# Expert 0's layers gathered ahead of batch 1, with its W2 and batch 1's q and k loads in another order

## The chip, the cores and the metric

The kernel runs on one core of one Trainium2 chip. The metric is the device time of one launch in microseconds (us). The kernel before was run three times: 1004.11, 1004.98 and 1006.6 us, median 1004.98.

## The reference

Two stages, all inputs in float32. First, sliding-window attention with a linear bias: 8 batches, 8 heads, 576 positions, 64 per head, a window of 128. Then a dense mixture of experts over the 4608 tokens of 512: every token goes through all 8 experts, and the gate's weights are balanced over rows and columns eight times.

```python
# attention, per batch and head
scores = q @ k.T / sqrt(64) - slope[h] * abs(i - j)      # only 0 <= i - j < 128
x[:, h] = softmax(scores) @ v                             # x: 4608 x 512
# mixture of experts
P = exp(x @ w_gate - max)                                 # 4608 x 8
repeat 8 times: P /= rowsum + 1e-9; P /= colsum + 1e-9; P *= 4608 / 8
out = sum over e of P[:, e] * (relu(x @ w1[e]) @ w2[e])   # w1: 512 x 1024, w2: 1024 x 512
```

## The kernel before

The kernel is one long program without loops on the chip: Python loops write every instruction in order, and each engine runs its own in that order, waiting on semaphores where data or a buffer isn't ready. It has two large parts. In the first, attention of the 8 batches is computed, and experts 0 and 1, which need no gate, are woven into it on TensorE as a filler. In the second, the gate is balanced and experts 2 to 7 are computed. The change touches the first part alone, and there the first two batches.

**Attention.** A batch has 4 full blocks of 128 positions and a tail of 64; each block is done in two half steps (`u`), four heads each, so a batch is ten half steps. `steps` lists them all; the main loop runs one half step each time round and already issues the scores, exps and masks of the next. In a half step TensorE makes the scores (`scores`, L438; both halves of a block together), ScalarE their exp (`exps`, L444), VectorE multiplies by the mask (`masks`, L449), TensorE multiplies by v (`values`, L472), VectorE takes the reciprocal of the sums (L482) and scales into `xsb` (L483). When a block is done, `turn_x` transposes x for the experts on TensorE (L510; batches 0 to 2 and 7), ScalarE or VectorE copies it out of PSUM (L519, L521), and `keep_x` stores x to memory (L498), at most three blocks late; that copy of x is read only in the second part.

**q, k and v.** `load_qk` loads q and k of a batch on SP's queue (L282; four loads of 512 KB for batches 1 and 2). `cast_qk` makes float16 of one of four head pairs `j`: k on ScalarE (L300), q on VectorE (L298), or both on POOL (L296). `turn_pe` then transposes on TensorE (L368), and ScalarE or VectorE copies k and q into place (L383, L381). `load_v` (L391) and `cast_v` (L403, L404, on POOL) bring one block of v each; v's raw tiles and the tails (`load_tail`, L271) share five buffers. In batch 0 three junk matmuls (`spin`, L260) go ahead of each `values`, and `spin_alone` adds some in other places.

**Experts 0 and 1.** `load_weights` loads W1 (L100) and W2 (L102) of an expert on POOL's queue. `unit_atoms` cuts a unit of two or four blocks of x into atoms: eight of layer 1 (four matmuls, L117, and a relu out of PSUM on ScalarE, L129; on alternating engines, L125 and L129, for blocks 0 to 3 of expert 0), and one atom of layer 2 for each block (eight matmuls, L141; two atoms of four for blocks 0 to 3 of expert 0). The result leaves PSUM on VectorE (`keep`: L553 for blocks 0 to 3 of expert 0, L559 for others). `order` lists the units; in the kernel before, expert 0's blocks 0 to 3 are two units of two blocks, all others have four.

`Filler` hands the atoms out. `take` gives out one, `fill(us)` several by an assumed cost of 0.87 us for each layer 1 atom of four blocks and 1.74 for a block of layer 2. `ready` says how many blocks of x exist, `allowed` which experts may start, and while `hold` is set no atom of layer 2 is given out. In the main loop a half step's share of the backlog is its `budget`; batch 0 has none. Between batches 0 and 1 (`nxt == (1, 0, 0)`) the loop gives out atoms by `take`, around the casts and turns of batch 1; between batches 1 and 2 it uses `fill`.

All PSUM tiles of this part other than scores come from one tag, `pmm`, with four banks: layer 1, layer 2, values, turns and gates share them.

**What sets the order around the change.** SP's queue, before: all of batch 0's loads, then q and k of batch 1 (L282), block 0 of v and the tail of batch 1, then one block of v for each finished block, with stores of x among them. POOL's queue, before: casts of v of batch 0 with W1 of expert 0 and the gate's weights among them, two casts of q of batch 1 (pairs 2 and 3), then W2 of expert 0, then casts of v of batch 1 as they land, with the weights of expert 1 at half step 5 of batch 0. `hold` is lifted at half step 2 of batch 1.

Of the kernel before, what the change touches and what calls it, by code (L numbers as in the profile page):

```python
# [14 lines left out]
def kernel(  # L15
# [10 lines left out]
    nc = tc.nc  # L26
# [4 lines left out]
    B, H, S, Dh = q.shape  # L31
# [5 lines left out]
    NBLK = Ntok // P  # L37
    NDT = HD // P
    NFT = Fd // P
    GT = 512  # L40
    NG = Ntok // GT
    NKB = 5
    RI = 4
# [18 lines left out]
    xd = nc.dram_tensor("xd", [NBLK, P, HD], FP16, kind="Internal").ap()  # L62
# [107 lines left out]
    L1_US, L2_US = 0.87, 1.74  # L170
# [62 lines left out]
    if True:  # L233
# [42 lines left out]
        def load_qk(b, parts=1):  # L276
            q32 = per.tile([P, H, RI * Dh], FP32, name=f"q32_{b}", tag="a8", bufs=8)
            k32 = per.tile([P, H, RI * Dh], FP32, name=f"k32_{b}", tag="a8", bufs=8)
            w = H // parts
            for n in range(parts):  # L280
                for t, src in ((q32, q), (k32, k)):
                    nc.sync.dma_start(  # L282
                        out=t[:, n * w : n * w + w],
                        in_=src[b, n * w : n * w + w, 0:SM, :].rearrange("h (p i) d -> p h (i d)", i=RI),
                    )
            raw[b] = (q32, k32)
# [126 lines left out]
        def sizes(kb):  # L413
            return P if kb < NKB - 1 else TL
# [85 lines left out]
        def turn_x(b, kb):  # L500
            nk = sizes(kb)
            blk = 4 * b + kb if kb < NKB - 1 else 4 * B + b // 2
            lo = 0 if kb < NKB - 1 else TL * (b % 2)
            xT, at = x_of(blk)
            to = xT[:, at, :, lo : lo + nk]
            xsb = xsbs.pop((b, kb))
            if by_pe(b):
                ps = aps.tile([P, NDT, P], FP16, name=f"psX_{b}_{kb}", tag="pmm", bufs=4)
                for j in range(NDT):
                    nc.tensor.matmul(  # L510
                        out=ps[:, j, 0:nk],
                        lhsT=xsb[0:nk, 2 * j : 2 * j + 2, :],
                        rhs=ident[0:nk, 0:nk],
                        is_transpose=True,
                        start=(j == 0),
                        stop=(j == NDT - 1),
                    )
                if b == 0:
                    nc.scalar.copy(out=to, in_=ps[:, :, 0:nk])  # L519
                else:  # L520
                    nc.vector.tensor_copy(out=to, in_=ps[:, :, 0:nk])  # L521
            else:
                nc.sync.dma_start(out=to, in_=xsb[0:nk].rearrange("p h d -> p (h d)"), transpose=True)
            kept.append((blk, lo, nk, xsb))
            keep_x(3)

        def gates(b0, b1):
# [31 lines left out]
            nc.vector.tensor_copy(out=yo, in_=ps)  # L559
            stores.append((e, blk, yo))  # L560

        order = [(0, 0, 2), (0, 2, 2)]
        for b0 in range(RI, NBLK, 4):
            order += [(0, b0, 4), (1, b0 - 4, 4)]
        order.append((1, NBLK - 4, 4))
        filler = Filler(
# [89 lines left out]
        load_first()  # L656
        spin_alone(20)
        make_mask(range(4))
        load_qk(1, 2)
        load_v(NKB)  # L660
        load_tail(1)
        cast_v(0)
        load_weights(0, 0, 1)
        cast_v(1)
# [11 lines left out]
        cast_v(2)  # L676
        nc.gpsimd.dma_start(out=wg_sb, in_=moe_w_gate.rearrange("(dt p) e -> p dt e", p=P))
        cast_v(3)
        cast_v(4)
        for j in (2, 3):  # L680
            cast_qk(1, j, (0,), True)
        load_weights(0, 1, 2)
        cast_qk(0, 2)
        cast_qk(0, 3)
        spin_alone(4)
# [8 lines left out]
        for n, (b, kb, u) in enumerate(steps):  # L694
            nxt = steps[n + 1] if n + 1 < len(steps) else None
            at = 2 * kb + u
            left = ((10 - at) % 10 + 1) if b >= XPE else 10 - at + 9 * (at == 9)
            budget = filler.backlog() / (11 if (b, at) == (XPE, 0) else left)
            if b == 0:
                budget = 0.0  # L700
            if nxt:
                if nxt[0] < XPE and nxt[1:] == (RI - 2, 1):
                    turn_pe(nxt[0], 0, NDT)
                if nxt == (1, 0, 0):
                    filler.ready = RI
                    spin_alone(6)
                    for _ in range(NFT):
                        filler.take()
                    cast_qk(1, 0)
                    cast_qk(1, 1)  # L710
                    for j in range(NDT):
                        turn_pe(1, 1, j)
                        turn_pe(1, 0, j)
                        if j < 2:
                            cast_qk(1, j + 2, (1,))
                        filler.take()
                if nxt == (2, 0, 0):
                    filler.fill(8.5)
                    cast_qk(2, 0)
                    cast_qk(2, 1)  # L720
                    filler.fill(2.5)
                    for j in range(NDT):
                        turn_pe(2, 1, j)
                        turn_pe(2, 0, j)
                        if j < 2:
                            cast_qk(2, j + 2, (1,))
                        filler.fill(1.0)
                if n == 0:
                    scores(*nxt)
                elif nxt[2] == 0 and nxt[1] < NKB - 1:  # L730
                    scores(*nxt)
                    scores(*nxt[:2], 1)
                if nxt[1] < NKB - 1:
                    exps(*nxt)
            if nxt and nxt[1] < NKB - 1:
                masks(*nxt)
            got = filler.fill(1.0) if b else 0.0
            if (b, kb, u) == (1, 1, 0):
                spin_alone(8)
            values(b, kb, u)  # L740
            if n > 0 and u == 0 and by_pe(steps[n - 1][0]):
                turn_x(*steps[n - 1][:2])
            if u == 1 and n // 2 + NKB < B * NKB:
                cast_v(n // 2 + NKB)
            filler.fill(budget - got)
            if at == 0 and b >= XPE:
                turn_tail(b)
            if at == 0 and b > XPE:
                filler.ready = 4 * b
            if at < 8 and b < XPE:  # L750
                filler.ready = 4 * b + at // 2
            if at == 8 and b < XPE:
                filler.ready = 4 * b + 4
            if u == 1 and not by_pe(b):
                turn_x(b, kb)
            if u == 1:
                if kb == 1 and b > 0:
                    gates(4 * b - 4, 4 * b)
                if n // 2 + NKB + 1 < B * NKB:
                    load_v(n // 2 + NKB + 1)  # L760
            if b == 0 and at == 5:
                load_weights(1)
            if (b, at) == (1, 8):
                filler.allowed.add(1)
            if (b, at) == (1, 5):
                for j in (2, 3):
                    cast_qk(2, j, (0,), True)
            if (b, at) == (1, 2):
                filler.hold = False
            if (b, at) == (0, 9):  # L770
                load_qk(2, 2)
            if (b, at) == (0, 7):
                homes(1)
            if (b, at) == (1, 3):
                homes(2)
            if 1 <= b < B - 2 and at == 3:
                load_qk(b + 2)
            if XPE <= b + 1 < B - 1 and at >= 8:
                cast_qk(b + 2, at - 8, (1,), True)
                cast_qk(b + 2, at - 8, (0,))  # L780
            if XPE <= b + 1 < B:
                if at == 0 and b + 1 == XPE:
                    for j in range(2):
                        cast_qk(b + 1, j, (1,), True)
                        cast_qk(b + 1, j, (0,))
                if at < 2:
                    cast_qk(b + 1, at + 2, (1,), True)
                    cast_qk(b + 1, at + 2, (0,))
                if at == 1:
                    store(1)  # L790
                    turn_qk(b + 1)
                    order_qk(b + 1, 1, range(NDT))
                if at == 5:
                    cast_tail(b + 1)
                if at in (6, 7):
                    order_qk(b + 1, 0, range(2 * at - 12, 2 * at - 10))
            if b < B - 1 and at == (1 if b > 1 else 5) and b:
                load_tail(b + 1)
            if 10 * b + at >= 66:
                i = 10 * b + at - 66  # L800
                if i % 8 == 0:
                    home_last(2 + i // 8)
                (load_w2 if i % 8 < 4 else load_w1)(2 + i // 8, i % 4, 4)
            if (b, at) == (7, 0):
                todo += sums_of(2, *extras(2))
            if b == 7 and at >= 5:
                some(1)
# [450 lines left out]
```

## Time and profile before

| | before |
|---|---|
| runs, us | 1004.11, 1004.98, 1006.6 (median 1004.98) |
| profiled execution, us | 1004.29 |
| its span, us | 1002.5 |
| TensorE busy, us | 989.1 |
| VectorE / ScalarE / POOL busy, us | 762.1 / 717.8 / 104.7 |
| granted TensorE clock | 1.00 |
| bytes moved by DMA | 122.46 MB, mean 122 GB/s |

The profile is of one execution; its span runs from the first to the last instruction, and 1.8 us of the run lie around it. Engines are PE (TensorE matmuls), PEld (TensorE weight loads), DVE (VectorE), ACT (ScalarE), POOL (GpSimd) and SP (which only issues DMAs). Lines of the order of time read: start, duration, engine, line of the kernel, operation, result tile <- operand tiles, shapes, count, and in brackets the idle time before it with what ended it. Durations of matmuls are those of single ones with their pipeline, so a run's length divided by its count gives the pace. A row "A <- B" in the waits means that A waited for B. In DMA views q1 is the queue that SP's loads and stores use, and q0 that of POOL's.

### The profile page before, as it was taken

What the parts mean: (1) busy time and instruction counts of PE and PEld (TensorE: products, weight loads), DVE (VectorE), ACT (ScalarE), POOL (GpSimd) and SP (SyncE); (2) the same over time, 40 slices, a digit from 0 to 9 for tenths busy, and PEclk for the clock granted to TensorE, in tenths of its full rate; (3) what the DMA queues carried; (4) which work ended last, traced back from release to release, by engine and by line L of the source; (5) the groups of instructions that cost most, each with busy time, mean ns of one, the idle gap of its engine ahead of it and who ended that gap; (6) DMA issues with size and microseconds to landing.
All of it is one profiled execution on the core that took longest, in us unless ns stands there. A gap on an engine that the chain in (4) does not pass through costs nothing.

```text
span 1002.5 us, 27939 instructions
## 1 busy us (share of the span) xinstructions
PE 989.1 (99%) x11591; PEld 801.5 (80%) x11591; DVE 762.1 (76%) x1598; ACT 717.8 (72%) x1216; POOL 104.7 (10%) x182
## 2 busy tenths in 40 slices
PE   7999999999999999999999999999999999999998
PEld 5645544445544899999999999999999999999997
DVE  6737676666688989887887887787787787787787
ACT  7654554555334768888888888888888888888885
POOL 3314344336010000000000000000000000000000
PEclk9999999999999999999999999999999999999999
DMA  9998788889998324324333334434433333433361
GB/s 250 212 261 226 158 217 225 216 182 191 237 187 170 75 50 99 79 61 98 80 64 96 80 70 86 85 68 84 87 82 66 96 75 67 99 75 65 96 117 48
DMA packets 264432, 122.46 MB, mean 122 GB/s; under 512 B 201969, under 2 KB 255729, under 8 KB 264305
## 3 DMA queue, kind: packets, MB, share of 16 engines
q1 hardware_dynamic: 249568, 102.68, 44.7%
q0 software_dynamic: 14304, 17.84, 10.6%
q8 instruction: 90, 1.47, 0.6%
q14 instruction: 38, 0.30, 0.1%
q10 hardware_dynamic: 432, 0.16, 0.1%
HBM read 78.30 MB, written 23.59 MB: 102 GB/s over the span
## 4 chain that ended last, share of the span: by engine, by line
PE 91%; DMA 3%; DVE 3%; ACT 1%; issue 0%; SPq 0%; POOL 0%; DVEq 0%
PE psM L1029 31%; PE psB L992 14%; PE psh L117 12%; PE psy L141 11%; PE psA L992 9%; PE psC L992 9%; DMA v<-in_v_dram 2%; PE psN L472 1%; PE psS L438 1%; DMA xT<-xsb 1%; PE psT L368 1%; DVE pt L449 0%; DMA q<-in_q_dram 0%; PE psG L531 0%; PE psh L971 0%
## 5 line engine op out<-in xcount | busy, mean ns | idle before, releaser
L1029 PEld LDWEIGHTS <-hs 128*128 128x128 f16 x2996 | 271.0, 98 | 22.4 <-DVE hs L1009 0.4
L1029 PE MATMUL psM<-w2l,hs 128*128 128x256 f16 x1440 | 186.6, 273 | 0.2 <-DVE hs L1009 0.2
L992 PEld LDWEIGHTS <-w1l 128*128 128x128 f16 x2848 | 181.4, 98 | 4.9 <-issue 0.5
L1005 ACT ACTIVATE hs<-hs 128x512 f16<-128x512 f16 x212 | 130.4, 630 | 35.3 <-DVE hs L1175 25.4
L1175 DVE TENSOR_TENSOR hs<-psB,s5y 128x512 f16<-128x512 f32 x106 | 73.3, 692 | 98.5 <-ACT xs L901 92.9
L992 PEld LDWEIGHTS <-s 128*128 128x128 f16 x2136 | 141.7, 98 | 6.4
L129 ACT ACTIVATE hT<-psh 128x512 f16<-128x512 f32 (+1 forms) x144 | 84.0, 586 | 78.9 <-PE psh L117 78.9
L117 PE MATMUL psh<-xT,w1t 128*128 128x512 f16 (+1 forms) x608 | 137.4, 368 | 2.5 <-DMA xT<-xsb 2.5
L901 ACT ACTIVATE xs<-xtok,L_sb 128x512 f16<-128x512 f16 x204 | 136.3, 721 | 1.8 <-DMA xset<-xs 1.8
L141 PE MATMUL psy<-w2t,hT 128*128 128x512 f16 x576 | 135.3, 379 | 0.0
L1029 PE MATMUL psM<-more,hs 128*128 128x256 f16 x864 | 129.5, 273 | 0.0
L992 PE MATMUL psA<-xset,w1l 128*128 128x128 f16 x1424 | 108.6, 219 | 0.0
L992 PE MATMUL psB<-xset,s 128*128 128x128 f16 x1424 | 108.6, 219 | 0.0
L444 ACT ACTIVATE pt<-psS 128x1024 f16<-128x1024 f32 x64 | 64.5, 1021 | 58.1 <-PE psS L438 57.6
L141 PEld LDWEIGHTS <-hT 128*128 128x128 f16 x576 | 53.5, 98 | 59.4 <-issue 1.7
L117 PEld LDWEIGHTS <-w1t 128*128 128x128 f16 x608 | 55.2, 98 | 55.4 <-issue 3.8
L1009 DVE TENSOR_TENSOR hs<-hs 128x1024 f16<-128x1024 f16 x107 | 73.9, 691 | 19.8 <-ACT hs L1005 17.7
L1166 ACT COPY psC<-psB 128x512 f32<-128x512 f32 x106 | 60.4, 570 | 38.8 <-PE psB L992 38.8
L449 DVE TENSOR_TENSOR pt<-pt,mask 128x1024 f16<-128x1024 f16 x64 | 49.2, 769 | 40.7 <-ACT pt L444 40.7
L559 DVE CAST yo<-psy 128x512 f16<-128x512 f32 x65 | 44.5, 689 | 44.7 <-PE psy L141 41.5
L1158 ACT COPY s5y<-psC 128x512 f32<-128x512 f32 x106 | 62.2, 587 | 22.7 <-PE psC L992 22.7
L1073 DVE TENSOR_TENSOR acc<-acc,psM 128x256 f32<-128x256 f32 (+1 forms) x162 | 73.9, 502 | 0.3
(127 smaller groups left out, 1421.0 us busy)
## 6 DMA issues: line engine op xcount, KB each, us to landing
s5y<-ysp SPq DMA_DIRECT2D x36, 256.0 KB, 3.0
ysp<-yo SPq DMA_DIRECT2D x65, 128.0 KB, 3.7
v<-in_v_dram SPq DMA_DIRECT2D x32, 256.0 KB, 4.7
out_dram<-acc SPq DMA_DIRECT2D x31, 256.0 KB, 2.5
q<-in_q_dram SPq DMA_DIRECT2D x5, 1024.0 KB, 6.5
k<-in_k_dram SPq DMA_DIRECT2D x5, 1024.0 KB, 8.8
xtok<-xd SPq DMA_DIRECT2D x34, 128.0 KB, 2.3
w2t<-in_moe_w_dram POOLq DMA_DIRECT2D x4, 1024.0 KB, 11.9
```

The lines of the kernel that those rows point to most:

```text
L117: nc.tensor.matmul(out=ps[:, 0:nt], lhsT=w1ts[e][:, dt, P * ft : P * ft + P], rhs=xT[:, at : at + nb, dt, :], start=(dt == 0), stop=(dt == ...
L129: nc.scalar.activation(out=st["hT"][:, ft, 0:nt], in_=ps[:, 0:nt], func=AF.Relu)
L141: nc.tensor.matmul(out=ps, lhsT=st["hT"][:, ft, P * ms : P * ms + P], rhs=w2ts[e][:, ft, :], start=(ft == 0), stop=(ft == NFT - 1),)
L444: nc.scalar.activation(out=pt, in_=ps.rearrange("p a y n -> p (a y) n"), func=AF.Exp, scale=scale)
L901: nc.scalar.mul(out=xs[2 * (n % 2) + m], in_=xtok[m], mul=P_sb[:, blk, e : e + 1])
L992: nc.tensor.matmul(out=ps[:, j, :], lhsT=q[k][:, P * j : P * j + P], rhs=xset[n % 2][:, x, P * k : P * k + P], start=(start and j == 0 and ...
L1005: nc.scalar.activation(out=h[n][:, slot], in_=src, func=AF.Relu)
L1009: nc.vector.tensor_tensor(out=t[:, 4:6], in0=t[:, 0:2], in1=t[:, 2:4], op=ALU.add)
L1029: nc.tensor.matmul(out=Ms[bk][:, half, :], lhsT=h[n][:, LEFT[m], f, :], rhs=W2L[e][RIGHT[m]][:, f, :], start=(e == 2 and f == 0 and half = ...
L1073: nc.vector.tensor_tensor(out=a, in0=a, in1=p2, op=op)
L1158: nc.scalar.copy(out=s5, in_=pc)
L1175: nc.vector.tensor_tensor(out=h[n][:, 3], in0=pb, in1=s5, op=ALU.add)
```

## The change

`order` now starts with expert 0's blocks 0 to 7 in four units of two blocks and expert 1's blocks 0 to 3 in one unit of four. W2 of expert 0 is asked for after the cast of block 3 of v of batch 0. q and k of batch 1 are no longer loaded at the start: at half step 7 of batch 0 SP gets a store of block 3 of x, which reads `xsb`, and behind it q and k of batch 1, blocks 0 and 1 of v, the tail and blocks 2 and 3 of v. POOL casts q's pairs 2 and 3 there; at half step 9 come the casts of v of batch 1, with the weights of expert 1 after the first two, and two more loads of v. The `turn_x` of that block of x no longer puts it in line for a store. Between batches 0 and 1 sixteen atoms are taken instead of eight, that is layer 1 of blocks 0 to 3; `hold` is lifted there; layer 2 of blocks 0 and 1 follows, then batch 1's turns with half a block of layer 2 after every second one.

```diff
-            kept.append((blk, lo, nk, xsb))
+            if (b, kb) != (0, RI - 1):
+                kept.append((blk, lo, nk, xsb))
...
-        order = [(0, 0, 2), (0, 2, 2)]
-        for b0 in range(RI, NBLK, 4):
+        order = [(0, 0, 2), (0, 2, 2), (0, 4, 2), (0, 6, 2), (1, 0, 4)]
+        for b0 in range(2 * RI, NBLK, 4):
             order += [(0, b0, 4), (1, b0 - 4, 4)]
...
         make_mask(range(4))
-        load_qk(1, 2)
-        load_v(NKB)
-        load_tail(1)
         cast_v(0)
...
         cast_v(3)
+        load_weights(0, 1, 2)
         cast_v(4)
-        for j in (2, 3):
-            cast_qk(1, j, (0,), True)
-        load_weights(0, 1, 2)
...
                     filler.ready = RI
                     spin_alone(6)
-                    for _ in range(NFT):
+                    for _ in range(2 * NFT):
                         filler.take()
+                    filler.hold = False
+                    filler.fill(2 * L2_US)
                     cast_qk(1, 0)
                     cast_qk(1, 1)
                     for j in range(NDT):
...
-                        filler.take()
+                        if j % 2:
+                            filler.take()
...
-            if u == 1 and n // 2 + NKB < B * NKB:
+            if u == 1 and b and n // 2 + NKB < B * NKB:
                 cast_v(n // 2 + NKB)
...
-                if n // 2 + NKB + 1 < B * NKB:
+                if b and n // 2 + NKB + 1 < B * NKB:
                     load_v(n // 2 + NKB + 1)
-            if b == 0 and at == 5:
+            if (b, at) == (0, 2 * RI - 1):
+                nc.sync.dma_start(out=xd[RI - 1], in_=xsbs[0, RI - 1].rearrange("p h d -> p (h d)"))
+                load_qk(1, 2)
+                load_v(5)
+                load_v(6)
+                load_tail(1)
+                load_v(7)
+                load_v(8)
+                for j in (2, 3):
+                    cast_qk(1, j, (0,), True)
+            if (b, at) == (0, 9):
+                cast_v(5)
+                cast_v(6)
                 load_weights(1)
+                load_v(9)
+                load_v(10)
+                for m in (7, 8, 9):
+                    cast_v(m)
...
-            if (b, at) == (1, 2):
-                filler.hold = False
```

`load_v(m)` and `cast_v(m)` count blocks through all batches, five to a batch: 5 to 9 are those of batch 1, 10 the first of batch 2.

## The prediction

> All times are microseconds of the one profiled execution of the kernel before (span 1002.5, whole run 1004.29, so 1.8 lies around the span). The median of the three runs shown is 1004.98, 0.7 above that run; I add my difference to the median. 0.3%, or 3 us, is about what a measurement of this kernel can tell from no change.
>
> **What bounds the kernel.** First the page: busy shares and the 40 slices.
>
> ```profile
> PE 989.1 (99%) x11591; PEld 801.5 (80%) x11591; DVE 762.1 (76%) x1598; ACT 717.8 (72%) x1216; POOL 104.7 (10%) x182
> ...
> PE   7999999999999999999999999999999999999998
> ```
>
> TensorE is busy 99% of the span. The built instruction orders of the two kernels show the same matmuls from the start of batch 3 on, so all the change can alter is what TensorE loses between 10 and 100 us. Busy is not full pace, though. So I read full-pace prices from the chain of waits and count the work of a stretch: a 256-column matmul of layer 1 is 0.110 (28 in 3.07), a 512-column one 0.216 (32 in 6.91), one of layer 2 0.216 (8 in 1.73), a q-and-k turn of one head pair 0.45, the scores of two half steps 0.54, the values of a half step 0.24, gates 0.38. Then the order of time on TensorE:
>
> ```profile
> 24.31 3.66 PE L117 MATMUL psh<-xT,w1t 128*128 128x256 f16 x32
> 28.51 0.70 PE L368 MATMUL psT<-ident,c 128*128 128x128 f16 x8 [0.55 <-ACT c L300]
> ...
> 32.62 0.70 PE L438 MATMUL psS<-qN,kN 64*128 64x256 f16 x8
> ...
> 39.39 1.04 PE L141 MATMUL psy<-w2t,hT 128*128 128x512 f16 x4
> ...
> 44.54 0.41 PE L472 MATMUL psN<-v,pt 128*128 128x65 f16 x8
> ...
> 49.27 1.89 PE L141 MATMUL psy<-w2t,hT 128*128 128x512 f16 x8
> 50.99 7.07 PE L117 MATMUL psh<-xT,w1t 128*128 128x512 f16 x32
> ```
>
> Layer 1 of expert 0 begins at 24.31, scores of batch 1 at 32.62, layer 2 only at 39.39 (W2, asked for at 28.36, landed at 39.2), and batch 1 is through at 49.27. From 24.31 to 50.99 the work is 7.0 (layer 1) + 6.9 (layer 2) + 2.0 (turns) + 2.2 (scores) + 2.2 (values) + 1.2 (spins) + 1.1 (turns of x) + 0.4 (gates) = 23.0, the elapsed time 26.7: **3.7 lost**. The windows view shows why the busy share hides it, and where else to look:
>
> ```profile
> 24.30:51.00 26.70, 25.41 (x302) 17.91 (x301) 20.44 (x50) 15.60 (x27) 8.55 (x20) 1.00 1.07 217
> 51.00:69.30 18.30, 18.30 (x111) 9.13 (x111) 6.64 (x11) 10.06 (x18) 2.69 (x7) 1.00 1.10 279
> 69.30:91.10 21.80, 21.39 (x198) 11.18 (x198) 13.07 (x31) 12.93 (x18) 6.08 (x13) 1.00 0.82 199
> ```
>
> Columns: elapsed, PE, PEld, DVE, ACT, POOL, granted clock, DMA share, GB/s. In the first stretch VectorE is 20.4 of 26.7 busy: attention's latency chain (exp 1.02, mask 0.69, reciprocal and scaling 0.6) is the limit, TensorE waits in small bits. From 51 to 69 TensorE is at full pace. From 69 to 91 about 1.65 is lost again (elapsed 21.8, work 20.2): exps queue behind eight evictions of 0.60, then a VectorE burst without a gap from 76.1 to 84.5. The whole prize is 3.7 + 1.65 = 5.3.
>
> **The change, part by part.**
>
> *Loads.* POOL now issues W2 of expert 0 at about 17.2 (after the cast of block 3 of v, before the wait for block 4) instead of 28.36. SP issues the store of x block 3 at 23.5 (its second half is written by 23.47), then the four q and k loads from 24.0 (0.5 each, as their rows show) instead of 13.2; v, tails and batch 2's loads follow. The DMA view:
>
> ```profile
> q1 hardware_dynamic: 1840, 1.59, 110.2%
> ...
> q0 software_dynamic: 608, 0.62, 73.0%
> q1 hardware_dynamic: 608, 0.61, 44.1%
> ```
>
> The first line is 22.5 to 27 us: q and k alone move 1.59 MB in 4.5 us, 354 GB/s. The other two are 53 to 58: weights (q0) and loads of SP (q1), both backlogged, move the same number of packets. W2 follows W1, which landed at 22.0; 1024 packets at 151 per us (755 in the window 31 to 36) are 6.8: about 28, needed at 31.3. q and k need 2.1 MB / 354 = 5.9 after a start near 25.8, plus 2 shared with W2: about 33.7; the last part is needed at 36. Both are covered, by some 2 to 3 us. v of batch 1 follows by 36 to 38 (needed from 41), expert 1's weights are asked for at about 37 instead of 40.58 and needed from 59; q and k of batch 2 land near 60 and are needed at 68. The delayed stores of x are read only by the last stage. The added wait is SP's, for VectorE's scaling at 23.47; behind it stand all those loads. On POOL the casts of q wait for their loads, and behind them stand the casts of v of batch 1 and expert 1's weights, which have the covers just named. Cost: 0, or one for one what a load is late (first rival). One term: block 4 of v landed at 22.49 beside W1, and now has W2 behind W1 as company; TensorE waits for it at 22.96. I take +0.2 (0 to 0.6).
>
> *Transition.* After layer 1's start come 64 matmuls of 0.110 (7.0) and 16 of layer 2 (3.45): 10.5. VectorE's order is then: evict block 0, evict block 1, cast q. The second eviction (0.69) starts when TensorE is done, the cast (0.56, from the row of two in 1.12) follows, so q's first turn waits 1.2 less 0.22 of k's turn and 0.1 of overlap: **0.9 lost, a new stall** where the old one of 0.55 was. Four turns (1.8), two halves of block 2 (1.73) and 0.2 for a PSUM bank: scores begin 15.1 after layer 1's start, against 8.3 now, for 6.94 more work: -0.1.
>
> *Batch 1.* From the first scores to the end of its last turn of x: now 16.65 for 14.2 of work, 2.45 lost. After the change 1.7 of filler is gone from the gaps between the third and fifth values (the listing shows none there). The chain of exp, mask and scaling stays: walking it with the rows' durations, the values of the sixth half step come 11.1 after the first scores (11.9 now). Then fillers return: eight 0.39 evictions on ScalarE share it with an exp of 1.02, while four PSUM banks are held by values waiting for VectorE: 0.4 lost; 7.95 to the end. Sum 19.05 for 15.95 of work, 3.1 lost: +0.65. Bounds: at batch 0's pace (7.4 from its second block's scores to the sixth values, mine 8.3) the term is -0.25, and -0.65 without the bank wait; at today's pace (9.1) and one exp (1.02) more in the way, +2.45. I keep the walk, whose pace lies between.
>
> *Two-block units.* 64 x 0.110 = 7.02 against 32 x 0.216 = 6.91: +0.1. ScalarE has 16 evictions of 0.386 for 8 of 0.598, +1.4; in the second unit each (0.39) fits under 0.44 of matmuls.
>
> *Batch 2.* Its layer 1 of expert 1 now runs ahead of the scores, so the exps no longer queue behind eight evictions, but the four casts of q of batch 3 still fall on VectorE in one go. Of 1.65 lost I take back 0.6 (between all of it, -1.65, and a worse burst, +0.3).
>
> Sum: +0.2 - 0.1 + 0.65 + 0.1 - 0.6 = **+0.25**, so 1004.5 in the profiled run's terms, 1005.3 on the median. All low ends together (the 0.9 and the bank wait gone too) give -3.2, all high ends +3.4.
>
> **Rivals.**
>
> *q and k come late (slower).* In the rows of before these 512 KB loads took 11.8 (q) and 12.0 (k) from issue to landing, and 16.0 for k beside expert 1's weights. The last is issued at 25.7: at 12 it lands at 37.7, at 16 at 41.7. It decides from 36 on: ScalarE must cast it (0.62) for the third turn, and TensorE, in order, waits one for one: +2.3 to +6.3, say 4, 1009. Against: then 2 MB of weights or four v blocks ran beside them; now one third of W2.
>
> *TensorE's rate falls in the thin half steps (slower).* From the third values to block 3's scores TensorE has 2.6 of work in some 4.5 us, without the spins that batch 0 has. The first 20 spins of the kernel took 3.77, 0.19 each against 0.11 later: one such spell costs 3.77 x (1 - 0.11/0.19) = 1.6, 1006.9. [...] Against: batch 0, with gaps of 0.81 and 0.55, shows a granted clock of 1.00, and no gap that I find is over 1 us.
>
> *The chain contracts (faster).* If batch 1 runs at batch 0's pace and the burst at 76 dissolves: 0.2 - 0.1 - 0.25 + 0.1 - 1.65 = -1.7; without the stall of 0.9 and the bank wait -3.0: 1003.3 to 1002.0. For: VectorE is the limit there and gets the same work in a longer time. Against: q's cast stands behind two evictions in its order.
>
> *The change doesn't do what it says* is excluded for the order (the listing shows W2, the store and the loads in their new places); W2 after 31.3 is priced like the first rival.
>
> **How the numbers follow.** Forecast 0.66, late loads 0.14, rate 0.06, contraction 0.14. Faster by over 3 us is half of the contraction and 0.01 of the forecast: 0.08. Slower by over 3 us is nearly all of late loads (0.13) and the forecast's high end (0.03): 0.16. The rest, 0.76, is within 0.3%. The range from 1002.4 to 1008.6 takes in the forecast's bounds but for the corners and the rate; it leaves out the far half of the contraction (0.07) and of late loads (0.07).
>
> **What would show it.** Right: layer 2 starting within 0.2 of the end of layer 1's 64 matmuls, without a wait for W2; a wait of 0.7 to 1.1 before the first q turn, put down to VectorE's cast; scores of batch 1 near 39.5; its end near 58.6; batch 3's first scores within 1 us of before. Wrong: TensorE waiting for a cast of k or POOL's cast of q; a granted clock under 1.00; batch 1 lasting under 17.5 or over 21 from its first scores.

## The result, and the profile after

The changed kernel ran 1011.77, 1014.13, 1017.11, 1010.92 and 1012.2 us: median 1012.2, where five runs of the kernel before gave a median of 1005.99. By the medians the change is slower by 6.2 us. The ratio with its 95% interval is 1.0083 (1.0066 to 1.01). It is an estimate of its own and not the quotient of the two medians (1.0062); by it the change is slower by 6.6 to 10 us. I forecast 1005.3 and a range from 1002.4 to 1008.6: the result lies outside it. The profiled execution (1011.77) has a span of 1009.9, 7.4 more than that of before.

The page of the changed kernel, the lines that answer to those of before:

```profile
PE 993.0 (98%) x11623; PEld 806.3 (80%) x11623; DVE 763.4 (76%) x1598; ACT 719.3 (71%) x1224; POOL 106.8 (11%) x182
...
PE   8989999999999999999999999999999999999998
```

TensorE is busy 3.9 us longer for the same work (the units of two make 32 matmuls more of half the size, and some matmuls ran slower) and idle 3.5 us longer. A slice is 25.2 us; the third, 50 to 76 us, has an 8 where the page of before has a 9. The order of time on TensorE there (columns as before):

```profile
24.96 7.15 PE L117 MATMUL psh<-xT,w1t 128*128 128x256 f16 x64
31.95 3.62 PE L141 MATMUL psy<-w2t,hT 128*128 128x512 f16 x16
...
37.09 0.84 PE L368 MATMUL psT<-ident,c 128*128 128x128 f16 x12 [1.30 <-DVE c L298]
...
40.88 0.61 PE L438 MATMUL psS<-qN,kN 64*128 64x256 f16 x8
...
52.40 1.03 PE L117 MATMUL psh<-xT,w1t 128*128 128x256 f16 x8 [1.20 <-DVE xT L521]
...
61.22 0.39 PE L510 MATMUL psX<-ident,xsb 128*128 128x128 f16 x4
62.78 1.47 PE L117 MATMUL psh<-xT,w1t 128*128 128x256 f16 x12 [1.18 <-DVE xT L521]
```

Up to 36 us it went as forecast: 64 matmuls of layer 1, layer 2 right behind them, no wait for W2. The stall of q's first turn came, at 1.30. New are the waits of **layer 1 for L521**: VectorE's copy of an x that TensorE has only just turned. Of TensorE's waits from 24 to 125 us it is the longest in total, and the kernel before has none of it:

```profile
PE psh L117 <- DVE xT L521: 3.6, 3, 1.2
```

The second such wait closes batch 1: x is turned by 61.6, the copy that layer 1 needs ends at 62.74. VectorE's own order shows what the copy stands behind:

```profile
61.18 0.69 DVE L560 CAST yo<-psy 128x512 f16<-128x512 f32 x1 [1.03 <-PE psy L141]
61.79 0.16 DVE L482 RECIPROCAL rden<-psN 64x4 f32<-64x4 f32 x1
61.98 0.42 DVE L483 TENSOR_TENSOR xsb<-psN,rden 64x256 f16<-64x256 f32 x1
62.33 0.41 DVE L521 COPY xT<-psX 128x512 f16<-128x512 f16 x1
```

The third wait, between batches 2 and 3, is followed by matmuls at a slower pace (12 in 3.67, where 12 of the same shape took 2.75 at 71.45), and the windows view shows the granted clock there (the column after POOL's):

```profile
108.98 1.60 PE L117 MATMUL psh<-xT,w1t 128*128 128x512 f16 x4 [1.18 <-DVE xT L521]
110.37 0.65 PE L472 MATMUL psN<-v,pt 128*128 128x65 f16 x8
110.83 3.67 PE L117 MATMUL psh<-xT,w1t 128*128 128x512 f16 x12
```
```profile
108.00:109.00 1.00, 0.02 (x1) 0.02 (x1) 0.97 (x5) 0.18 (x1) 0.00 (x0) 1.00 1.16 322
109.00:110.00 1.00, 1.00 (x4) 0.37 (x4) 0.86 (x2) 0.00 (x0) 0.00 (x0) 0.64 1.21 307
110.00:111.00 1.00, 1.00 (x11) 0.69 (x10) 0.00 (x0) 0.32 (x1) 0.00 (x0) 0.50 1.16 328
111.00:112.00 1.00, 1.00 (x4) 0.30 (x2) 0.91 (x3) 0.27 (x1) 0.80 (x2) 0.50 0.78 208
112.00:113.00 1.00, 1.00 (x4) 0.40 (x3) 0.09 (x1) 0.24 (x1) 0.94 (x2) 0.66 1.20 313
```

TensorE is idle for nearly all of 108 to 109 while VectorE is busy for 0.97 of it; then 3.41 us follow at half clock (0.50, from 109.28 to 112.69), which cost about 1.7 (3.41 x 0.5, an estimate).

**Where the time went.** With the full-pace prices of the prediction I count what each stretch lost (elapsed time less work), before and after:

| stretch | lost before | lost after | difference |
|---|---|---|---|
| start of the kernel to layer 1 (elapsed) | 24.31 | 24.96 | +0.65 |
| transition: from there to the last values of batch 0 (they follow the first scores of batch 1) | 1.34 | 1.92 | +0.58 |
| batch 1: from there to its last values | 2.45 | 6.19 | **+3.74** |
| batch 2: from there to the first values of batch 3 | 1.57 | 4.61 | **+3.04** |
| later, to the end of the span (what is left) | | | -0.7 |

With 0.1 of more work for the units of two they sum to the 7.4. The two large entries hold the three waits for L521 (3.6 in all) and the half clock (1.7).

**The theory to test (theory 1).** Counting the matmuls of L117 and L141 in the built order, at their full-pace prices, 5.3 us of filler are given out ahead of the last values of batch 0 in the kernel before, and 12.2 in the changed one, of 13.9 that blocks 0 to 3 have. The rest, a block of layer 2, goes before the first block's second values of batch 1, and the store is then empty. Between these and the third block's second values, before gives out 2.6 us of old filler (four matmuls of layer 2 each at 39.39, 41.38 and 43.67); the changed kernel has only 0.9 of layer 1 (two atoms) on a block just turned, which waits. **An empty store makes every next filler the newest one, and that stands in the latency chain of VectorE.** At the end of batch 2 it is the same: one block of layer 2 (1.73) that stands there in the kernel before, behind the scores of batch 3, is already spent. The lines of the kernel before:

```profile
41.38 1.03 PE L141 MATMUL psy<-w2t,hT 128*128 128x512 f16 x4
...
43.67 1.04 PE L141 MATMUL psy<-w2t,hT 128*128 128x512 f16 x4
...
100.25 0.61 PE L438 MATMUL psS<-qN,kN 64*128 64x256 f16 x8
100.79 1.90 PE L141 MATMUL psy<-w2t,hT 128*128 128x512 f16 x8
```

Rivals: theory 2, the order of the loads is the cause; theory 3, the units of two blocks are.

### The profile page after: what moved, and what is told of

The parts are those of the page before. It is cut to its first block, busy times and chain, and to the rows that moved or that the text cites. A ratio compares the mean times of both kernels' runs of the same rounds, so it can differ in the third digit from the quotient of the medians.

```text
span 1009.9 us, 28012 instructions
## 1 busy us (share of the span) xinstructions
PE 993.0 (98%) x11623; PEld 806.3 (80%) x11623; DVE 763.4 (76%) x1598; ACT 719.3 (71%) x1224; POOL 106.8 (11%) x182
## 4 chain that ended last, share of the span: by engine, by line
PE 91%; DVE 4%; DMA 2%; ACT 2%; issue 1%; DVEq 0%; ACTq 0%
PE psM L1042 32%; PE psB L1005 14%; PE psh L117 12%; PE psy L141 11%; PE psA L1005 9%; PE psC L1005 9%; PE psN L472 1%; PE psS L438 1%; DMA xT<-xsb 1%; ACT pt L444 1%; DMA k<-in_k_dram 1%; DVE pt L449 1%; PE psh L984 1%; DVE xsb L483 1%; PE psT L368 0%
## 5 line engine op out<-in xcount | busy, mean ns | idle before, releaser
L117 PE MATMUL psh<-xT,w1t 128*128 128x512 f16 (+1 forms) x640 | 139.2, 360 | 5.7 <-DVE xT L521 3.6
L141 PE MATMUL psy<-w2t,hT 128*128 128x512 f16 x576 | 135.1, 379 | 0.0
L117 PEld LDWEIGHTS <-w1t 128*128 128x128 f16 x640 | 58.9, 99 | 56.7 <-issue 9.2
L141 PEld LDWEIGHTS <-hT 128*128 128x128 f16 x576 | 53.7, 98 | 59.0 <-issue 1.5
```

Source lines behind the costliest of these rows:

```text
L117: nc.tensor.matmul(out=ps[:, 0:nt], lhsT=w1ts[e][:, dt, P * ft : P * ft + P], rhs=xT[:, at : at + nb, dt, :], start=(dt == 0), stop=(dt == ...
L141: nc.tensor.matmul(out=ps, lhsT=st["hT"][:, ft, P * ms : P * ms + P], rhs=w2ts[e][:, ft, :], start=(ft == 0), stop=(ft == NFT - 1),)
```

## The experiments

The ratios of e1 to e15 are against runs of the kernel before on the same chip (its medians were 1005.5 to 1006.2); like the first, they are not quotients of the medians. None is slower by as much as 2%. "Clock" is the mean granted clock over the timed runs.

| run | median, us | ratio (95%) | clock |
|---|---|---|---|
| changed kernel | 1012.2 | 1.0083 (1.0066 to 1.01) | 0.9976 |
| e1 W2 early | 1009.16 | 1.0045 (1.0028 to 1.0062) | 0.9976 |
| e2 units of two | 1004.87 | 0.9995 (0.9985 to 1.0006) | 0.9996 |
| e3 gathered | 1015.88 | 1.011 (1.0088 to 1.0132) | 0.9945 |
| e4 x copy on ScalarE | 1007.65 | 1.0021 (1.0009 to 1.0034) | 0.9998 |
| e5 loads late | 1011.9 | 1.0065 (1.005 to 1.0079) | 0.9963 |
| e6 layer 2 back | 1007.25 | 1.0015 (1.0001 to 1.0029) | 0.9986 |
| e7 units of four | 1013.29 | 1.0068 (1.005 to 1.0085) | 0.9953 |
| e8 two and W2 between | 1005.86 | 0.9999 (0.9985 to 1.0014) | 0.9989 |
| e9 reserve | 1006.12 | 1.0005 (0.9994 to 1.0017) | 0.9998 |
| e10 two and reserve | 1005.81 | 0.9999 (0.9987 to 1.0011) | 0.9994 |
| e11 three mends | 1009.11 | 1.0034 (1.002 to 1.0049) | 0.9988 |
| e12 spins in the gap | 1013.33 | 1.0084 (1.006 to 1.0108) | 0.9985 |
| e13 early q and k | 1007.21 | 1.0017 (1.0007 to 1.0026) | 0.999 |
| e14 back and ScalarE | 1006.45 | 1.0007 (0.9989 to 1.0025) | 0.9989 |
| e15 back and reserve | 1006.43 | 1.0011 (0.9996 to 1.0026) | 0.9991 |

### The parts alone, and the copy moved

**e1**, the kernel before with W2 ahead:

```diff
         cast_v(3)
+        load_weights(0, 1, 2)
         cast_v(4)
...
-        load_weights(0, 1, 2)
```

> The kernel before with one thing changed: W2 of expert 0 is asked for ahead of the cast of block 4 of v and of the casts of q and k of batch 1 (whose loads stay at the top); half steps, units and hold as before. Theory 1 (fillers run dry, and layer 1 then waits for VectorE's copy of an x just turned): the store of fillers is untouched, so 1005 to 1008 us, no wait of layer 1 for the copy of x between 24 and 120 us, about +1 from q and k that share the queues with W2. Theory 2 (the order of the loads is the cause): most of the loss is here, 1010 to 1013.

1009.16: above what theory 1 allowed. The order of the loads does cost something by itself, ahead of batch 1 and not in it (no wait for L521 from 24 to 125 us). ScalarE's order shows k of batch 1 late beside W2:

```profile
31.52 0.62 ACT L300 CAST c<-k 128x512 f16<-128x512 f32 x1 [1.05 <-DMA k<-in_k_dram]
```

TensorE's turn behind it waits 0.94, the transition loses 1.15 more than before; the rest of this profile's difference is 0.9 at the start and a longer wait at 138 us (2.76 for a DMA's x, 1.27 before) with 3.4 us at half clock behind it (0.50, from 141.1 to 144.6).

**e2**, the kernel before with units of two:

```diff
-        order = [(0, 0, 2), (0, 2, 2)]
-        for b0 in range(RI, NBLK, 4):
+        order = [(0, 0, 2), (0, 2, 2), (0, 4, 2), (0, 6, 2), (1, 0, 4)]
+        for b0 in range(2 * RI, NBLK, 4):
```

> The kernel before with one thing changed: blocks 4 to 7 of expert 0 are two units of two blocks instead of one of four. Theory 1: 1005 to 1007.5, since layer 2 of blocks 0 to 3 still stands in the half steps of batch 1 and layer 1 comes to a new block only when its copy is long done; any wait of layer 1 for the copy of x is under 0.5 us. Theory 3 (units of two blocks are the cause, by smaller tiles and by starting on newer blocks): 1009 to 1013, with waits of about 1.2 us at block 5 or block 7 of batch 1.

1004.87, and no wait for L521 up to 125 us: theory 3 falls. Its one new wait is for W2, asked for at 28.97:

```profile
41.32 1.04 PE L141 MATMUL psy<-w2t,hT 128*128 128x512 f16 x4 [1.18 <-DMA w2t<-in_moe_w_dram]
```

**e3**, the kernel before with W2 ahead and the gathering:

```diff
-                    for _ in range(NFT):
+                    for _ in range(2 * NFT):
                         filler.take()
+                    filler.hold = False
+                    filler.fill(2 * L2_US)
...
-                        filler.take()
+                        if j % 2:
+                            filler.take()
...
-            if (b, at) == (1, 2):
-                filler.hold = False
```

> The kernel before with W2 early (as in the run with that alone) and the gathering: both units of layer 1 in one run ahead of batch 1, the hold lifted there and layer 2 put behind it, then a filler for every second turn; loads of q, k and v at the top, units of four blocks. Theory 1: 1009 to 1013, since the store of fillers is spent before batch 1; batch 1 has little to fill with, and layer 1 waits about 1 us for VectorE's copy of block 7 or of block 11. Theory 2 and theory 3: within 1 us of the run with W2 early alone, 1005 to 1008.

1015.88, more than theory 1's high end. The profile is of the slowest of its six runs (1020.44). The largest part of its loss is where theory 1 puts it: no filler at all from 50.3 to 61.7 us, when block 7 has been turned and copied. It loses 2.9 to a wait for W2, and layer 1 begins 2.8 later than before. In batch 1 it loses 9.1 (before 2.45), and the granted clock falls to half for 6.8 us there:

```profile
58.00:60.00 2.00, 1.43 (x28) 1.12 (x29) 1.93 (x7) 0.17 (x1) 0.00 (x0) 0.93 1.16 249
60.00:62.00 2.00, 1.03 (x8) 0.44 (x6) 1.60 (x6) 0.00 (x0) 0.00 (x0) 0.50 1.11 327
62.00:64.00 2.00, 2.00 (x6) 0.73 (x5) 0.00 (x0) 0.32 (x1) 0.00 (x0) 0.50 1.13 325
64.00:66.00 2.00, 2.00 (x7) 0.64 (x5) 0.00 (x0) 0.88 (x2) 0.40 (x1) 0.50 0.77 193
```

**e4**, the changed kernel with the copy of x elsewhere:

```diff
-                if b == 0:
+                if b < XPE:
                     nc.scalar.copy(out=to, in_=ps[:, :, 0:nk])
```

> The changed kernel with one thing altered: the copy of a turned x goes to ScalarE in batches 1 and 2 too (as it does in batch 0), not to VectorE. Theory 1: the three waits of layer 1 for that copy shrink to under 0.5 us each, so 3 to 5 us come back: 1007 to 1009.5. If a late x itself (its turn or its product) and not VectorE's queue is what layer 1 waits for, or if the loads or the units are the cause, 1011 to 1013, or slower where ScalarE's exponentials are delayed.

1007.65, 4.6 less than the changed kernel. Of its waits from 24 to 125 us, one is left for the copy, and the granted clock is 1.00 in 10 of 12 runs. The profile loses 1.65 less than the changed kernel's in batch 1 and 2.4 less in batch 2. In batch 1 that is less than half of the 3.74. From 24 to 125 us TensorE still waits 0.8 for the masks, 0.6 for the scaling, and for the copy as ScalarE now makes it:

```profile
PE psh L117 <- ACT xT L519: 0.7, 1, 0.7
```

### The parts taken back

**e5** is the kernel before with the loads of the change alone: W2 early, and q, k and v late behind the store of x.

> The kernel before with the loads alone as in the change: W2 of expert 0 early, q, k and v of batch 1 behind the store of x; half steps, hold and units as before. In the changed kernel q of batch 1 came at 33.7 us, and here only half of layer 1, until about 28.6, covers it. Theory 1: the loss is in one place, a wait of 3 to 6 us ahead of the first turns of batch 1, with perhaps a stretch at half clock; batch 1 and batch 2 lose no more than before (no wait of layer 1 for the copy of x): 1009 to 1014. Theory 2 (the order of the loads is what costs the changed kernel its time, in batch 1 and 2 too): 1010 to 1014 with waits inside batch 1 or 2 as in the changed kernel.

1011.9, and the loss stands where theory 1 puts it: ahead of batch 1 there is only half of layer 1 as cover, and TensorE waits for k.

```profile
25.73 3.66 PE L117 MATMUL psh<-xT,w1t 128*128 128x256 f16 x32
35.11 1.03 PE L368 MATMUL psT<-ident,c 128*128 128x128 f16 x8 [5.72 <-ACT c L300]
```

ScalarE's cast waited 5.06 for k's load until 34.44; the granted clock is 0.50 from 31.5 to 38.3. Batch 1 and batch 2 lose 2.55 and 0.98, no more than before. So the late loads need more cover than half of layer 1, and the changed kernel paid for it out of the store.

**e6**, the changed kernel less one line:

```diff
                     filler.hold = False
-                    filler.fill(2 * L2_US)
```

> The changed kernel without the line that runs layer 2 of the four blocks (7 us) ahead of batch 1; the hold stays lifted, so layer 2 is taken between the turns and in the half steps of batch 1. Theory 1: the store is back; TensorE waits up to 2.5 us for q ahead of the first turns (which layer 2 covered), but the three waits of layer 1 for the copy of x in batches 1 and 2 shrink or go, and with them the stretch at half clock at 109 us: 1007 to 1010. Theory 2 and theory 3 (loads, or units of two): 1011 to 1014, the waits for the copy of x as in the changed kernel.

The line is worth two blocks of layer 2, 3.45 us, not the 7 that the expectation names. Without it 1007.25: **5 of the 6 us are back**. The whole list of TensorE's waits from 24 to 125 us has no L521:

```profile
PE psT L368 <- ACT c L300: 1.4, 2, 0.8
PE psX L510 <- DVE xsb L483: 0.3, 1, 0.3
```

Batch 1 now loses 2.3 and batch 2 1.65, as before (2.45 and 1.57), with the loads late and the units of two still in place. What is left is the wait for k, 1.4 in all (0.55 of it as before), which layer 2 had covered.

**e7** is the changed kernel with the kernel before's `order`.

> The changed kernel with blocks 4 to 7 of expert 0 as one unit of four blocks. Theory 1: with the store spent, batch 1 has no filler at all until block 7 is turned; TensorE idles in its half steps (as in the gathered run: 6.6 us more lost in batch 1, part of it at half clock), so slower than the changed kernel, 1013 to 1017. Theory 3 (units of two are the cause): faster than the changed kernel, 1005 to 1010.

1013.29, with its interval overlapping that of the changed kernel: that it is slower is not shown. With e2 it shows that units of two are no cause. Batch 1 loses 9.1, as in e3, and 6.8 us of it run at half clock (0.50, from 54.9 to 61.8); batch 2 loses 1.0.

**e8** is the kernel before with units of two and W2 asked for behind the cast of block 4 of v (at 23.60, where e1 has it at 21.53).

> The kernel before with units of two blocks (as in the run with those alone) and W2 of expert 0 asked for just ahead of the casts of q and k of batch 1, behind the cast of block 4 of v: a place between that of the kernel before and that of the run with W2 early. It would take away the wait for W2 of 1.18 us at 41.3 us that the run with units of two shows. Theory 1: nothing runs dry, 1003.5 to 1006.5, and the least of all if k does not come later. Theory 2 (W2 ahead of q and k costs by itself): 1007 to 1010, with a wait of about 1 us for k of batch 1 as in the run with W2 early.

1005.86, no wait for W2, none for k beyond the 0.5 of before, but one of 1.59 for v: no gain that can be measured.

### Mends, and what they left open

**e9** and **e10** keep a reserve, in the kernel before and with units of two:

```diff
-            left = ((10 - at) % 10 + 1) if b >= XPE else
+            left = ((10 - at) % 10 + 2) if b >= XPE else
```

> The kernel before with one number changed: from batch 3 on the fillers are spread over one half step more, so that the store is never quite empty where a batch ends (in the kernel before TensorE waits 1.27 us at 136.8 us for the x of block 15, just turned, with nothing else to do). Theory 1, carried over (an empty store makes the next filler the newest one, which waits): layer 2 of older blocks stands in that place, the wait goes, and with it the stretches at half clock that some runs have there; 1003 to 1005.5, granted clock 1.00 in nearly all runs. If the wait there is worth nothing, or comes back as another: 1005 to 1007.

> As the run with the reserve alone, and with units of two blocks, which gave 0.9995 of the kernel before. Theory 1: 1002.5 to 1005, the fastest of these if the two add up; otherwise 1005 to 1007.

Both missed: 1006.12 and 1005.81, the same as before, though the granted clock came out as expected in e9 (1.00 in 10 of 12 runs). In e9 the wait at 137 us is gone (0.1 lost there instead of 1.45), but in the half step behind it TensorE loses 0.93, most of it (0.76) in another wait for a transposed x, and further on 0.66; two waits of values for VectorE's scaling, 0.5 each, are new as well. The gain turned into other waits.

**e11** has e6's, e4's and e9's edits on the changed kernel.

> The changed kernel with what theory 1 says it lacks: layer 2 left in the half steps of batch 1, the copy of x on ScalarE in batches 1 and 2, and the reserve from batch 3 on. Theory 1: 1004 to 1006.5, that is, nothing of the loss is left but some 1 us of waiting for q and k ahead of batch 1. If the order of the loads has a cost of its own further on: 1007 to 1010.

1009.11, missed. Three more runs were made for that.

**e13**: e6's order of the layers in the kernel with units of two, but q, k and v loaded at the top, W2 as in e8. **e14**: e6 and the copy on ScalarE. **e15**: e6 and the reserve.

> The run with layer 2 put back, but with q, k and v of batch 1 loaded at the top as in the kernel before, and W2 asked for behind the cast of block 4 of v: layer 1 of blocks 0 to 3 in one run, units of two, hold lifted ahead of batch 1. If the rest of that run's loss (1.3 us on the medians; a wait of 1.4 us for k of batch 1) is the late loads: that wait falls to about 0.5 as before, and 1004.5 to 1006.5. If it is the run of layer 1 by itself, or layer 2 waits for W2 in turn: 1006.5 to 1009, with a wait for W2 of 1 to 3 us between the turns of batch 1.

> The run with layer 2 put back (1007.25), and the copy of x on ScalarE in batches 1 and 2. With the store back no layer 1 waits for that copy, so moving it buys nothing: 1006 to 1008. If this move is what made the mended kernel slower than that run (ScalarE's exponentials behind copies): 1008.5 to 1010.

> The run with layer 2 put back (1007.25), and the reserve of fillers from batch 3 on. The reserve alone gave 1.0005 of the kernel before, so here too nothing: 1006 to 1008.5. If the reserve is what made the mended kernel slower than that run: 1008.5 to 1010.

e14 (1006.45) and e15 (1006.43) clear both mends: neither costs anything that can be measured. e13 gave 1007.21: with the loads early the wait for k is 0.55 as before, but layer 2, taken between the turns, now waits for W2:

```profile
36.10 1.04 PE L141 MATMUL psy<-w2t,hT 128*128 128x512 f16 x4 [2.30 <-DMA w2t<-in_moe_w_dram]
```

What the late loads cost is uncertain from run to run. Up to batch 1's turns e6, e14 and e15 are the same program, and the first turn of k waited 0.55 in e6 and e15, but in e14:

```profile
36.08 1.14 PE L368 MATMUL psT<-ident,c 128*128 128x128 f16 x16 [3.22 <-ACT c L300]
```

The 48 runs of e6, e11, e14 and e15 spread from 1004.3 to 1011.8, the 12 of e13, with early loads, from 1006.0 to 1008.7. That this uncertain landing is why e11's median came out above the others fits, and is not shown: e11's own profile (1006.77) has the short wait.

**e12**, the changed kernel with spins in the third wait:

```diff
+            if (b, at) == (2, 9):
+                spin_alone(10)
             got = filler.fill(1.0) if b else 0.0
```

> The changed kernel with ten extra matmuls on constants (about 1 us at full clock) put into the third wait, ahead of layer 1 of blocks 8 to 11, where TensorE idles 1.2 us and the granted clock then falls to half for 3.41 us. If that idling brings the stretch on: no stretch at 109 us, mean granted clock of the runs up from 0.998 to 0.999 or more, and 1 to 2 us less: 1010 to 1011.5. If the stretch has another origin: as the changed kernel, 1011.5 to 1014.

1013.33, in the range that was named for another origin of the stretch: no time came back. In the profile the place itself did as the expectation's first case says, and 109 to 110 is at full clock:

```profile
109.00:110.00 1.00, 1.00 (x9) 0.57 (x7) 1.00 (x4) 0.00 (x0) 0.00 (x0) 1.00 1.20 330
```

Batch 2 loses 2.3 less than in the changed kernel. But from 143 us on, in the same execution, the start of batch 4 lost 4.3, where the changed kernel's profile lost 1.1 there: a wait of 2.5 for a transposed x. The mean granted clock of that execution is 0.998, as much as one stretch of 3.41 us at half clock takes off (3.41 x 0.5 / 1012 = 0.0017, an estimate), and from 107 to 115 us it is 1.00. One profile of each can't say whether the spins moved the stretch or missed it.

## Why the prediction was wrong

The terms were to add up to +0.25, which on the median is 1005.2; the 1005.3 is a slip of rounding.

- **Loads**: right. W2 was there for layer 2, q was there at 33.67 for POOL (I had 33.7 for q and k; the third pair of k came at 35.1 in e6), and TensorE waited for neither in the changed kernel's profile. The rival of late q and k did not happen there. It is real where the cover is less (5.72 in e5), and in e14, whose program is the same up to the end of layer 1, the first k landed only at about 35.4 (an estimate: its turn at 36.08 less the 0.67 from k's landing to the turn in e5), when ScalarE had it by 32.1 in the changed kernel: the landing differs between executions by about as much as the 2 to 3 us of cover that I counted.
- **Block 4 of v**, +0.2 (0 to 0.6): layer 1 began 0.65 later. e2, whose start is the kernel before's, began 0.69 later in its profile, so this is not put down to the change.
- **Transition**, -0.1: +0.58 in lost time. The new stall was there with the cause that I named, at 1.30 where I had 0.9: q's first cast took 0.83, not the 0.56 that I took from a row of two. Scores began 15.9 after layer 1, not 15.1.
- **Batch 1**, +0.65, high end +2.45: **the step that failed**. The table has +3.74 for it. I had seen that no filler stands between the third and fifth values, and walked the chain of exp, mask and scaling; then I let "fillers return". I never asked which: they are layer 1 of blocks 5 and 7, turned a moment ago, and VectorE's copy of them was not in the walk. From the first scores to the last turn of x it took 20.7, where I had 19.05: +2.3 in the term's own stretch, still under its high end. The other wait of 1.18 comes right behind that stretch, and no term had it. e4 and e6 show it from both sides: the copy moved, 4.6 back; older filler put in its place, 5 back.
- **Units of two**, +0.1: right (e2, 0.9995). With a spent store they even bring the first new filler forward; e7 without them loses 9.1 in batch 1 instead of 6.2.
- **Batch 2**, -0.6 (high end +0.3): +3.04, for the same reason, and the second term that left the copy out. The burst did shrink a little, as I had argued (the lost time up to the fifth block of batch 2 is 0.95 against 1.46), but at its end the store was one block of layer 2 short, layer 1 waited for block 11's copy, and 1.7 went to the half clock.
- **TensorE's rate**, a rival at 0.06 and 1.6: a lower rate came, in another place than I looked, and on top of the waits: a granted clock of 0.50 for 3.41 us at the end of batch 2, while the half steps of batch 1 ran at 1.00. That thin half steps lower the rate was not shown by the profile of before; the 1.6 was my estimate from the pace of the first 20 spins. In e3 and e7 the clock did fall to 0.50 in batch 1, for 6.8 us. By the mean clocks of the runs (0.9976, and 0.999 over the runs of before) it is some 0.0014 x 1010 = 1.4 of the 6.2. A run of the changed kernel at clock 1.00 still took 1010.92.

The range failed with the step: I bounded batch 1 by the pace of the chain alone, not by what TensorE would be given to do in it, and batch 2 with no wait for the copy at all.

## What to carry to other kernels

Work woven into gaps is a store, and it has to last through the latency-bound stretch: running it early, where TensorE had no gap, takes it from where the gaps are. When a filler is moved, ask what stands in its old place next; if that is the newest data, the producer's last copy is on the path. And a load that is moved behind needs its own cover: here two covers (for the loads and for batch 1) were paid from one store.

## What the runs showed of the hardware

In the changed kernel's profile the granted clock fell to 0.50 for 3.41 us (109.28 to 112.69), 0.3 behind the end of a wait of 1.18 us (from 107.8 to 109.0 TensorE is busy for 0.02), with TensorE busy for 3.26 of the 3.4 us before. The length of the wait alone does not decide it: the two waits for L521 ahead of it in the same profile (1.20 and 1.18) were followed by full clock (1.00 from 46 to 109 us), and so was the 3.22 in e14 (16 turns behind it took 1.14, where 8 took 1.03 at half clock in e5; the mean clock of that execution is 1.0). What does decide it, no run here shows.

In e3, e5 and e7 the stretch was 6.8 us, twice 3.41: in e5 (31.5 to 38.3) it began within a wait of 5.72 (29.4 to 35.1), in e3 and e7 in half steps without filler whose single waits were at most 1.1. Runs of one kernel differ in their mean clock: of the 24 runs of the kernel before beside e1 to e4, the eleven at 1.00 averaged 1004.8, the nine at 0.998 averaged 1006.5, two at 0.999 1005.5 and two at 0.996 1007.9. One stretch takes 3.41 x 0.5 / 1005 = 0.0017 off the mean, by my estimate, and the changed kernel's profiled execution, with one such stretch, has a mean of 0.998.
